# An attention and soft-MoE kernel: weight fetches behind the query stacks, and a new order of the first pair

## The chip, the cores and the metric

One core of one Trainium2 chip. The metric is the device time of one execution in microseconds (us). Engines: TensorE (PE, its weight loads PEld), VectorE (DVE), ScalarE (ACT), GpSimd (POOL) and SyncE (SP), which here only issues DMAs.

## The reference

Three layers follow each other, all in float32.

- Attention: q, k, v are 4 batches x 8 heads x 576 positions x 64. q and k are rotated (RoPE), then `softmax(q k^T / 8) v`.
- Soft MoE on the 2304 x 512 result x: `logits = x phi` (32 slots), softmax over the tokens for the dispatch and over the slots for the combine; 8 experts of 4 slots, each `relu(s w1) w2` with 512 x 1024 and 1024 x 512 weights.
- A feed-forward layer: `h = x w_in` (512 x 2048), `g = h tanh(softplus(h))`, `g w_out`.

## The kernel before, in words

The program is fully unrolled. It has an attention part (to about 325 us), a part for the experts (to about 370 us) and the feed-forward layer, whose second product fills the rest. The change touches the attention part alone.

**Pairs.** Attention runs over 16 pairs of heads (NP = 16), one after the other in a software pipeline. A pair has nine score tiles `S0` to `S8`: tile t of 128 queries of head h is number 2t + h, and S8 holds the last 64 positions of both heads. For each tile TensorE writes scores to PSUM (`S`, `scores` L375), VectorE takes the row maximum (`M`, `maxima` L383), ScalarE the exponential (`E`, `expo` L389), TensorE transposes it (`T`), ScalarE or VectorE copies it out (`t`), and TensorE multiplies by v (`A`, `B`). The pool `ps_s` (L79) has two score banks, so a score tile waits until the exponential of an earlier one has freed its bank. The pool `ps_m` (L80) has four banks for all else.

**High and low parts.** Scores are computed from two float32r parts of q and k, a high part (a rounded copy) and a low part (the rest), stacked on the 128 partitions. For pairs after the first, rotated q and k (GpSimd, `ropek`, `ropeq`) are transposed by TensorE (`Hk`, `Hq`, and `G` for the last 64 positions), ScalarE writes the high parts to the tile `parth` (`hka`, `hqa`, `ga`), VectorE the low parts to `partl` (`hkd`, `hqd`, `gd`), and DMAs from SBUF to SBUF carry them to their places in `qk_st` and `k2_st`: steps `dk` (eight DMAs) and `dq` (four), from `stack` L337. There is one buffer of `parth` and one of `partl`, so that `ga` (`rem_hi` L310), which is the first to write `parth` for the pair after, waits until all stacks that read it have landed.

**The first pair.** It has no stacks: the parts are written straight from PSUM (L718 to L773). `xk` holds both heads' transposed keys in one tile (heads on partitions 0 to 63 and 64 to 127) in one of the two score banks, `xq` the queries, `xr` the last 64 queries. `hi` (L728) is a ScalarE activation, `lo` (L731) a VectorE operation that needs the high part. Reads of one PSUM tile by two engines take turns in program order. `busy(n)` (L718) issues n filler matmuls.

**Order.** Each engine executes its instructions in the order in which the program issues them (class `InOrder`, L82). That order is written by hand: `PLAN` (L28) for each period, where `name@n` is the step for the pair n periods back, and `PLAN0` (L38) for the first pair. A step that issues to several engines takes its place in each of their queues. SyncE's queue carries nearly all DMAs: the stacks, the loads of q, k (`ld`) and v (`lv`), and, in most pairs, blocks of w_in and w_out that ScalarE, VectorE and GpSimd convert on the side (`ci` load, `Ca` ScalarE, `Cb` VectorE, `Cs` GpSimd, `co` store).

**The weight fetch.** Step `wf` (L820) is `fetch(ahead.pop(0), behind=True)`: one DMA of 1 MB of expert weights into a tile that nothing else uses by then, kept in its place in the order. It runs once a period for eight pairs, p = 2 to 9, as `wf@2`. In the old `PLAN` it stands between `hqa` and `Cb1`, so on SyncE's queue behind `dk` and in front of `dq`.

```python
             "wf": lambda p: fetch(ahead.pop(0), behind=True) if 2 <= p < 2 + NRA else None,
```

Of the kernel before, what the change touches and what calls it, by code (L numbers as in the profile page):

```python
# [27 lines left out]
PLAN = (  # L28
# [7 lines left out]


PLAN0 = (  # L38
    "E0 w3 Hk w3 ci1 S2 M2 S4 hka E2 M4 T0 S1 t0 E4 hkd M1 G S3 T2 ga E1 gd dk M3 S6 t2 E3 M6 T1 S5 E6 Hq t1 M5 "
    "T3 S7 hqa E5 hqd dq t3 M7 K0 S8 k0 E7 M8 A0 E8 ld:1 ropek:1 z0 A1 A2 ropeR:1 A3 A4 T4 ropeq:1 x0 t4 T5 "  # L40
    "ld:2 Y0 y0 t5"
).split()

# [5 lines left out]
def kernel(  # L49
# [14 lines left out]
    NB, H, S, D = q.shape  # L64
# [6 lines left out]
    SCALE = 1.0 / float(D) ** 0.5  # L71
# [282 lines left out]
    def s_mm(p, s, qc, h):  # L354
        st = qk_st[p % 2]
        for half in range(2):
            o = h * S + half * 288
            pe.matmul(s[:, half, 0:288], lhsT=st[:, qc:qc + 128], rhs=st[:, KC + o:KC + o + 288],
                      start=True, stop=False)
            pe.matmul(s[:, half, 0:288], lhsT=st[:, qc:qc + 128], rhs=k2_st[p % 2][:, o:o + 288],  # L360
                      start=False, stop=True)

    def s_mm2(p, s):
        st = qk_st[p % 2]
        for half in range(2):
            n = 0
            for o, qc in ((half * 288, QZ), (KB + half * 288, QBR)):
                for rhs in (st[:, KC + o:KC + o + 288], k2_st[p % 2][:, o:o + 288]):
                    pe.matmul(s[:, half, 0:288], lhsT=st[:, qc:qc + 128], rhs=rhs,
                              start=(n == 0), stop=(n == 3))  # L370
                    n += 1
# [3 lines left out]
    def scores(p, i):  # L375
        t, h = divmod(i, 2)
        s = sc[p, i] = ps_s.tile([128, 2, 512], F32, tag="s", name="s")
        if t < 4:
            s_mm(p, s, (QA, QB)[h] + t * 128, h)
        else:  # L380
            s_mm2(p, s)

    def maxima(p, i):  # L383
        if i == 0:
            stat[p] = [a4.tile([128, 10], F32, tag="nmax", name="nmax", bufs=2), zs[p % 2],
                       a4.tile([128, 10], F32, tag="rz", name="rz", bufs=2)]
        dve.tensor_reduce(out=stat[p][0][:, i:i + 1], in_=sc[p, i][:, :, 0:288], axis=AX.XY, op=ALU.max, negate=True)
# [322 lines left out]
    up, dn = slice(0, 64), slice(64, 128)  # L710
    xk = ps_s.tile([128, 2, 512], F32, tag="s", name="xk").rearrange("p a n -> p (a n)")
    xq = ps_m.tile([128, 512], F32, tag="m", name="xq")
    xr = ps_m.tile([128, R], F32, tag="m", name="xr")
# [4 lines left out]
    def busy(n):  # L718

        z = c_all[:, 0, 0:4].rearrange("p t s -> p (t s)")  # L720
        for _ in range(n):
            pe.matmul(none, lhsT=z, rhs=z, start=True, stop=True)
# [5 lines left out]
    def hi(out, ps, scale=1.0):  # L728
        act.activation(out=out, in_=ps, func=AF.Copy, scale=scale)

    def lo(out, ps, hi, scale=1.0):  # L731
        dve.scalar_tensor_tensor(out=out, in0=ps, scalar=scale, in1=hi.bitcast(F32), op0=ALU.mult, op1=ALU.subtract)
# [12 lines left out]
    ka, k2a = st[:, KC:KC + S], s2[:, 0:S]  # L745
    kb, k2b = st[:, KC + KB:KC + KW], s2[:, KB:KW]
    kf, k2f = st[:, KC + S:KC + KB], s2[:, S:KB]
    qa, qar, qb = st[:, QA:QA + 512], st[:, QAR:QA], st[:, QB:QB + S]
    hi(ka[up], xk[up, 0:S])
    hi(k2a[dn], xk[up, 0:S])  # L750
    hi(k2b[dn], xk[dn, 0:S])
    hi(kb[up], xk[dn, 0:S])
    hi(qa[up, 0:128], xq[up, 0:128], SCALE)
    hi(qa[up, 128:512], xq[up, 128:512], SCALE)
    lo(k2a[up], xk[up, 0:S], ka[up])
    lo(ka[dn], xk[up, 0:S], ka[up])
    lo(qa[dn, 0:128], xq[up, 0:128], qa[up, 0:128], SCALE)
    busy(9)
    scores(0, 0)
    lo(qa[dn, 128:512], xq[up, 128:512], qa[up, 128:512], SCALE)  # L760
    hi(qb[dn, 0:512], xq[dn, 0:512], SCALE)
    hi(k2f[dn], xk[dn, 512:S])
    hi(kf[up], xk[dn, 512:S])
    hi(qb[dn, 512:S], xr[dn])
    hi(qar[up], xr[up])
    maxima(0, 0)
    lo(kb[dn], xk[dn, 0:S], k2b[dn])
    lo(k2b[up], xk[dn, 0:S], k2b[dn])
    lo(kf[dn], xk[dn, 512:S], k2f[dn])
    lo(k2f[up], xk[dn, 512:S], k2f[dn])  # L770
    lo(qb[up, 512:S], xr[dn], qb[dn, 512:S])
    lo(qar[dn], xr[up], qar[up])
    lo(qb[up, 0:512], xq[dn, 0:512], qb[dn, 0:512], SCALE)  # L773
    for i in range(2):
        dma(out=phi_sb[64 * i:64 * i + 64, :, i], in_=phi.rearrange("(c h p) s -> h p c s", h=2, p=64)[i])
    load_v(1)
# [101 lines left out]
    begin = [((w + ":0").split(":")[0], int((w + ":0").split(":")[1])) for w in PLAN0]  # L878
    late_feed = [(n, 1) for n in ("G", "ga", "gd", "Hk")]
    steps["w3"] = lambda p: busy(3)  # L880
    for name, p in begin:
        steps[name](p)
    for period in range(1, NP + last):
        for name, n in plan:
            p = period - n
# [445 lines left out]
```

## Time and profile before

| | |
|---|---|
| median of 3 runs | 607.21 us (604.88 to 607.4) |
| the profiled execution's own time | 606.94 us |
| its span, first to last instruction | 604.8 us |
| TensorE busy | 584.4 us, 97% |
| VectorE, ScalarE, GpSimd busy | 383.9, 339.2, 218.2 us |
| bytes moved by DMA | 108.46 MB, 179 GB/s over the span |

Times in rows are microseconds from the span's start. A busy share is an average over stages; TensorE's matmuls are pipelined and drawn longer than the distance at which they follow each other. "idle before <- X" names what ended an engine's idle time, as inferred from semaphores; a DMA's time to landing counts from its issue.

### The profile page before, as it was taken

The numbers are of one execution on the slowest core, as the hardware profiler recorded it, in microseconds if no ns is written. First come the engines' busy times: TensorE is split into PE (matmuls) and PEld (weight loads), VectorE is DVE, ScalarE is ACT, GpSimd is POOL, SyncE is SP. The second block draws the span as 40 slices with busy tenths as digits, with TensorE's granted clock in tenths as the row PEclk, the third lists the DMA queues.
The fourth block names the chain that finished last, engine by engine and source line by source line (L and its number), as shares of the span: only waits on it lengthen the run. The fifth ranks groups of instructions, "written<-read, shape, count | busy, mean of one in ns | idle before, by whom it ended". The sixth has DMA issues, their size and how long they took to land.

```text
span 604.8 us, 11027 instructions
## 1 busy us (share of the span) xinstructions
PE 584.4 (97%) x3949; PEld 461.2 (76%) x3949; DVE 383.9 (63%) x813; ACT 339.2 (56%) x778; POOL 218.2 (36%) x267
## 2 busy tenths in 40 slices
PE   8899999999999999999998989999999999999996
PEld 7688887877878787787875435778788888888885
DVE  6688888977869786887654243887865333433332
ACT  4688887877879686886761023767662111222221
POOL 4967889578875877673000300000000000000000
PEclk9999999999999999999998999999999999999999
DMA  8598789989999889769759798424002000210004
GB/s 230 148 249 223 218 233 288 272 242 257 267 265 242 243 259 276 203 172 299 258 216 362 268 388 354 174 98 147 2 29 77 0 1 0 68 37 1 2 1 104
DMA packets 59398, 108.46 MB, mean 179 GB/s; under 512 B 13008, under 2 KB 25424, under 8 KB 58832
## 3 DMA queue, kind: packets, MB, share of 16 engines
q1 hardware_dynamic: 59072, 107.50, 60.3%
q8 instruction: 31, 0.51, 0.4%
q10 hardware_dynamic: 272, 0.26, 0.1%
q14 instruction: 23, 0.19, 0.1%
HBM read 70.25 MB, written 9.96 MB: 133 GB/s over the span
## 4 chain that ended last, share of the span: by engine, by line
PE 74%; DMA 5%; DVE 3%; ACT 1%; POOL 1%; issue 1%; SPq 0%; DVEq 0%; ACTq 0%
PE o_ps L1215 32%; PE s L90 9%; PE m_av L90 9%; PE t L90 6%; PE hp L1181 3%; DMA qk_st<-parth 3%; PE h_ps L1008 2%; PE so_ps L1077 2%; PE warm L583 2%; PE m_lg L90 1%; DMA qk_st<-partl 1%; PE m_x L90 1%; PE m_si L90 1%; DMA w<-in_q_dram 1%; PE m_q L90 1%; PE m_wp L1158 1%
## 5 line engine op out<-in xcount | busy, mean ns | idle before, releaser
L90 DVE TENSOR_REDUCE nmax<-s 128x1 f32<-128x576 f32 x144 | 106.8, 751 | 24.9 <-PE s L90 22.9
L90 ACT ACTIVATE P<-s,nmax 128x576 f32<-128x576 f32 x144 | 107.1, 745 | 18.1 <-DVE nmax L90 16.3
L1215 PE MATMUL o_ps<-wo_h,gh 128*128 128x512 f32 x288 | 113.0, 392 | 0.0
L1215 PE MATMUL o_ps<-wo_l,gh 128*128 128x512 f32 x288 | 113.0, 392 | 0.0
L90 PE MATMUL s<-qk_st 128*128 128x288 f32 x320 | 102.6, 337 | 5.7 <-ACT P L90 5.0
L1188 ACT ACTIVATE room<-hp 128x512 f32<-128x512 f32 x72 | 43.0, 599 | 106.6 <-PE hp L1181 102.0
L1215 PE MATMUL o_ps<-wo_h,gl 128*128 128x512 f32 x288 | 100.8, 391 | 0.9 <-DVE gl L1196 0.9
L90 PE MATMUL s<-k_st,qk_st 128*128 128x288 f32 x320 | 89.3, 295 | 0.0
L90 POOL TENSOR_TENSOR w<-w,cs 128x512 f32<-128x512 f32 (+2 forms) x75 | 87.6, 1187 | 4.4 <-DMA w<-in_k_dram 2.3
L90 PE MATMUL t<-cs,P 128*128 128x128 f32 x576 | 84.2, 273 | 0.4 <-ACT P L90 0.4
L90 PEld LDWEIGHTS s<-qk_st 128*128 128x128 f32 x320 | 60.3, 188 | 21.7 <-ACT P L90 9.5
L90 POOL TENSOR_TENSOR w<-w 128x256 f32<-128x256 f32 (+2 forms) x86 | 65.4, 781 | 18.5 <-ACT P L90 15.9
L1190 DVE CAST gh<-room 128x512 fp32r<-128x512 f32 x49 | 20.9, 427 | 79.4 <-ACT room L1188 79.3
L90 PEld LDWEIGHTS t<-cs,P 128*128 128x128 f32 x576 | 68.1, 142 | 1.5 <-ACT P L90 0.7
L90 ACT COPY PT<-t 128x512 f32<-128x512 f32 (+1 forms) x111 | 60.9, 557 | 12.9 <-PE t L90 12.1
L1215 PEld LDWEIGHTS o_ps<-wo_h,gl 128*128 128x128 f32 x288 | 54.0, 188 | 13.2 <-DVE gl L1196 1.7
L1215 PEld LDWEIGHTS o_ps<-wo_l,gh 128*128 128x128 f32 x288 | 54.4, 189 | 9.0 <-DVE wo_l L1068 0.2
L1215 PEld LDWEIGHTS o_ps<-wo_h,gh 128*128 128x128 f32 x288 | 54.1, 188 | 9.2
L90 PEld LDWEIGHTS s<-k_st,qk_st 128*128 128x128 f32 x320 | 60.6, 190 | 0.0
L1196 DVE TENSOR_TENSOR gl<-room,gh 128x512 fp32r<-128x512 f32 x72 | 49.6, 690 | 4.6
L90 PE MATMUL m_av<-PT,w 128*64 128x320 f32 (+1 forms) x384 | 52.0, 411 | 0.0
L90 POOL TENSOR_TENSOR c_all<-c_all,tmp 128x64 f32<-128x64 f32 (+1 forms) x44 | 21.6, 490 | 53.0 <-DVE tmp L90 51.2
(171 smaller groups left out, 843.4 us busy)
## 6 DMA issues: line engine op xcount, KB each, us to landing
w<-in_moe_w_dram SPq DMA_DIRECT2D x23, 1024.0 KB, 8.0
w<-in_moe_w_dram SPq DMA_DIRECT2D x36, 256.0 KB, 5.4
w<-in_moe_w_in_dram SPq DMA_DIRECT2D x16, 512.0 KB, 5.5
qk_st<-parth SPq DMA_DIRECT2D x45, 144.0 KB, 5.3
qk_st<-partl SPq DMA_DIRECT2D x45, 144.0 KB, 5.5
room<-in_moe_w_out_dram SPq DMA_DIRECT2D x12, 512.0 KB, 3.5
w<-in_q_dram SPq DMA_DIRECT2D x16, 256.0 KB, 3.8
w<-scr_in SPq DMA_DIRECT2D x4, 1024.0 KB, 6.4
```

The lines of the kernel that those rows point to most:

```text
L90: return lambda *a, **k: tc.keep_in_program_order(f(*a, **k))
L583: tc.keep_in_program_order(nc.tensor.matmul(ps, lhsT=ident, rhs=ident, start=True, stop=True))
L1008: tc.keep_in_program_order(nc.tensor.matmul(h_ps[32 * g:32 * g + 32, fh, :], lhsT=si_t[:, c, 32 * e:32 * e + 32], rhs=rows[g][:, cc * F1 + ...
L1077: tc.keep_in_program_order(nc.tensor.matmul(so_ps[32 * g:32 * g + 32, :], lhsT=h_t[eg][:, c, 32 * g:32 * g + 32], rhs=parts[2, e, hf][0][: ...
L1158: pin(nc.tensor.matmul(ps[32 * c:32 * c + 32, :], lhsT=s_t[:, c, :], rhs=wi[:, c, :], start=True, stop=True))
L1181: pin(nc.tensor.matmul(hp[:, x, :], lhsT=wst[:, f * 128:(f + 1) * 128], rhs=ct[:, i * 256:(i + 1) * 256], start=True, stop=True))
L1188: pin(nc.scalar.activation(out=gg, in_=hp, func=AF.Mish))
L1190: pin((nc.scalar.copy if 0 < u < NG * GR else nc.vector.tensor_copy)(gh, gg))
L1196: pin(nc.vector.tensor_tensor(out=gl, in0=gg, in1=gh.bitcast(F32), op=ALU.subtract))
L1215: pin(nc.tensor.matmul(ops[i, n], lhsT=g_[:, cols], rhs=w_[f], start=(j == 0 and (x, k) == (0, 0)), stop=(j == NG - 1 and all(y[0] != n fo ...
```

## The change

- In `PLAN`, `wf@2` moves from behind `hqa` to behind `dq`.
- In the first pair's code, head 0's low parts come directly after head 0's two high parts; head 1's high parts follow behind S0, and the filler matmuls in front of S0 go from nine to six.
- The rest of head 1's parts becomes six steps of `PLAN0`: `hx` and `hr` (high parts of the last keys and queries), `lk`, `lf`, `lr`, `lq` (low parts of keys, last keys, last queries, queries).
- `PLAN0` takes the score tiles in the order 0, 2, 4, 6, 1, 3, 5, 7, 8 where it had 0, 2, 4, 1, 3, 6, 5, 7, 8. The second `w3` (three filler matmuls) moves from in front of S2 to behind S4, `ci1` from in front of S2 to behind S6, and the other steps keep their places around the tiles they belong to.

```diff
@@ -28,7 +28,7 @@
 PLAN = (
     "S0 y0@1 Cs0@1 E8@1 ropek@-1 hka t5@1 M0 Z@2 ci0 T6@1 hkd S1 R@1 zz@2 K1@1 ropeR@-1 co0@1 dk "
     "M1 t6@1 E0 rA@1 rD@1 E1 X0@1 k1@1 w0@1 ca0@1 T7@1 S2 t7@1 Ca1@1 Hq Q@1 M2 S3 M3 qD@1 hqa "
-    "wf@2 Cb1@1 qA@1 B0@1 E2 B1@1 E3 B2@1 B3@1 B4@1 D@1 S4 z1@1 x1@1 hqd Ca0 Cs1@1 T3 M4 X1@1 dq "
+    "Cb1@1 qA@1 B0@1 E2 B1@1 E3 B2@1 B3@1 B4@1 D@1 S4 z1@1 x1@1 hqd Ca0 Cs1@1 T3 M4 X1@1 dq wf@2 "
     "t3 w1@1 T0 S5 dD@1 M5 Y1@1 t0 y1@1 Cb0 co1@1 dA@1 lv@1 ca1@1 T2 T1 E4 rb@1 rc@1 rd@1 t2 S6 K0 T4 M6 ci1 E5 "
     "lC@1 t1 La S7 Lb ra k0 G@-1 t4 E6 A0 la z0 A1 lb ropeq@-1 ro A2 M7 A3 lA A4 x0 ga@-1 lB "
     "S8 ld@-2 gd@-1 T5 E7 M8 Y0 Hk@-1 "
@@ -36,8 +36,8 @@
 
 
 PLAN0 = (
-    "E0 w3 Hk w3 ci1 S2 M2 S4 hka E2 M4 T0 S1 t0 E4 hkd M1 G S3 T2 ga E1 gd dk M3 S6 t2 E3 M6 T1 S5 E6 Hq t1 M5 "
-    "T3 S7 hqa E5 hqd dq t3 M7 K0 S8 k0 E7 M8 A0 E8 ld:1 ropek:1 z0 A1 A2 ropeR:1 A3 A4 T4 ropeq:1 x0 t4 T5 "
+    "hx E0 lk lf w3 Hk S2 hr M2 S4 E2 M4 lr w3 hka E4 lq S6 ci1 S1 T0 hkd M6 G t0 M1 S3 T2 ga E6 gd dk E1 M3 t2 S5 E3 T1 "
+    "Hq t1 M5 T3 S7 hqa E5 hqd dq t3 M7 K0 S8 k0 E7 M8 A0 E8 ld:1 ropek:1 z0 A1 A2 ropeR:1 A3 A4 T4 ropeq:1 x0 t4 T5 "
     "ld:2 Y0 y0 t5"
 ).split()
 
@@ -748,29 +748,38 @@
     qa, qar, qb = st[:, QA:QA + 512], st[:, QAR:QA], st[:, QB:QB + S]
     hi(ka[up], xk[up, 0:S])
     hi(k2a[dn], xk[up, 0:S])
+    lo(k2a[up], xk[up, 0:S], ka[up])
+    lo(ka[dn], xk[up, 0:S], ka[up])
+    hi(qa[up, 0:128], xq[up, 0:128], SCALE)
+    hi(qa[up, 128:512], xq[up, 128:512], SCALE)
+    lo(qa[dn, 0:128], xq[up, 0:128], qa[up, 0:128], SCALE)
+    busy(6)
+    scores(0, 0)
+    lo(qa[dn, 128:512], xq[up, 128:512], qa[up, 128:512], SCALE)
     hi(k2b[dn], xk[dn, 0:S])
     hi(kb[up], xk[dn, 0:S])
-    hi(qa[up, 0:128], xq[up, 0:128], SCALE)
-    hi(qa[up, 128:512], xq[up, 128:512], SCALE)
-    lo(k2a[up], xk[up, 0:S], ka[up])
-    lo(ka[dn], xk[up, 0:S], ka[up])
-    lo(qa[dn, 0:128], xq[up, 0:128], qa[up, 0:128], SCALE)
-    busy(9)
-    scores(0, 0)
-    lo(qa[dn, 128:512], xq[up, 128:512], qa[up, 128:512], SCALE)
     hi(qb[dn, 0:512], xq[dn, 0:512], SCALE)
-    hi(k2f[dn], xk[dn, 512:S])
-    hi(kf[up], xk[dn, 512:S])
-    hi(qb[dn, 512:S], xr[dn])
-    hi(qar[up], xr[up])
     maxima(0, 0)
-    lo(kb[dn], xk[dn, 0:S], k2b[dn])
-    lo(k2b[up], xk[dn, 0:S], k2b[dn])
-    lo(kf[dn], xk[dn, 512:S], k2f[dn])
-    lo(k2f[up], xk[dn, 512:S], k2f[dn])
-    lo(qb[up, 512:S], xr[dn], qb[dn, 512:S])
-    lo(qar[dn], xr[up], qar[up])
-    lo(qb[up, 0:512], xq[dn, 0:512], qb[dn, 0:512], SCALE)
+
+    def head_1(what):
+        if what == "hx":
+            hi(k2f[dn], xk[dn, 512:S])
+            hi(kf[up], xk[dn, 512:S])
+        elif what == "hr":
+            hi(qb[dn, 512:S], xr[dn])
+            hi(qar[up], xr[up])
+        elif what == "lk":
+            lo(kb[dn], xk[dn, 0:S], k2b[dn])
+            lo(k2b[up], xk[dn, 0:S], k2b[dn])
+        elif what == "lf":
+            lo(kf[dn], xk[dn, 512:S], k2f[dn])
+            lo(k2f[up], xk[dn, 512:S], k2f[dn])
+        elif what == "lr":
+            lo(qb[up, 512:S], xr[dn], qb[dn, 512:S])
+            lo(qar[dn], xr[up], qar[up])
+        else:
+            lo(qb[up, 0:512], xq[dn, 0:512], qb[dn, 0:512], SCALE)
+
     for i in range(2):
         dma(out=phi_sb[64 * i:64 * i + 64, :, i], in_=phi.rearrange("(c h p) s -> h p c s", h=2, p=64)[i])
     load_v(1)
@@ -878,6 +887,7 @@
     begin = [((w + ":0").split(":")[0], int((w + ":0").split(":")[1])) for w in PLAN0]
     late_feed = [(n, 1) for n in ("G", "ga", "gd", "Hk")]
     steps["w3"] = lambda p: busy(3)
+    steps |= {n: lambda p, n=n: head_1(n) for n in ("hx", "hr", "lk", "lf", "lr", "lq")}
     for name, p in begin:
         steps[name](p)
     for period in range(1, NP + last):
```

## Rows read from the trace of the kernel before

**Rows 1.** The page's chain by engine; windows table (busy us, clock, transfers, GB/s).
```profile
PE 74%; DMA 5%; DVE 3%; ACT 1%; POOL 1%; issue 1%; SPq 0%; DVEq 0%; ACTq 0%
...
130.00:155.00 25.00, 23.92 (x190) 19.17 (x187) 18.78 (x43) 19.78 (x48) 17.55 (x23) 1.00 0.98 248
```

**Rows 2.** Waits of ScalarE, 80 to 260 us (total, times, longest); its timeline.
```profile
ACT parth L90 <- DMA qk_st<-partl: 4.2, 2, 2.4
ACT parth L90 <- DMA qk_st<-parth: 3.2, 3, 1.5
...
143.00 0.37 ACT L90 CAST parth<-m_rem 128x256 fp32r<-128x256 f32 x1 [1.81 <-DMA qk_st<-partl]
```

**Rows 3.** Timeline of TensorE (start, us, ..., idle before and what ended it).
```profile
84.72 0.61 PE L90 MATMUL m_k<-cs,w 128*128 128x128 f32 x4
85.08 0.38 PE L90 MATMUL s<-qk_st 128*128 128x288 f32 x1
...
144.16 0.40 PE L90 MATMUL s<-qk_st 128*128 128x288 f32 x1 [0.92 <-ACT P L90]
...
145.56 0.40 PE L90 MATMUL s<-qk_st 128*128 128x288 f32 x1 [0.15 <-DMA w<-in_q_dram]
...
181.85 0.66 PE L90 MATMUL m_k<-cs,w 128*128 128x128 f32 x4 [0.58 <-ACT lt L90]
...
182.75 0.40 PE L90 MATMUL s<-qk_st 128*128 128x288 f32 x1 [0.24 <-ACT P L90]
...
240.90 0.40 PE L90 MATMUL s<-qk_st 128*128 128x288 f32 x1 [1.49 <-ACT P L90]
...
242.50 0.40 PE L90 MATMUL s<-qk_st 128*128 128x288 f32 x1 [0.36 <-ACT P L90]
```

**Rows 4.** Timeline of SyncE, DMA issues from 131.9 us on.
```profile
131.91 0.62 SPq L154 DMA_DIRECT2D w<-in_moe_w_dram  x1
132.63 0.84 SPq L90 DMA_DIRECT2D qk_st<-parth  x1
```

**Rows 5.** DMA issues: KB each, us to landing; issued at 134.16, at 76.50.
```profile
qk_st<-parth SPq DMA_DIRECT2D x1, 144.0 KB, 8.7
...
qk_st<-parth SPq DMA_DIRECT2D x1, 144.0 KB, 4.4
```

**Rows 6.** Conversion loads issued at 182.44 and 174.78 (us to landing); ScalarE's readers.
```profile
w<-in_moe_w_in_dram SPq DMA_DIRECT2D x1, 512.0 KB, 7.2
...
w<-in_moe_w_in_dram SPq DMA_DIRECT2D x1, 512.0 KB, 9.0
...
186.62 1.23 ACT L90 ACTIVATE w<-w 128x512 f32<-128x512 f32 x2
...
190.74 1.26 ACT L90 ACTIVATE w<-w 128x512 f32<-128x512 f32 x2
```

**Rows 7.** First pair, timelines: three rows of ScalarE, three of VectorE, two of TensorE.
```profile
10.16 0.65 ACT L90 ACTIVATE qk_st<-xk 64x576 fp32r<-64x576 f32 x1
...
18.14 0.74 ACT L90 ACTIVATE P<-s,nmax 128x576 f32<-128x576 f32 x1 [2.48 <-DVE nmax L90]
...
27.74 0.74 ACT L90 ACTIVATE P<-s,nmax 128x576 f32<-128x576 f32 x1 [0.73 <-DVE rz L90]
...
10.84 0.75 DVE L90 SCALAR_TENSOR_TENSOR k_st<-xk,qk_st 64x576 fp32r<-64x576 f32 x1 [1.01 <-ACT qk_st L90]
...
15.77 0.23 DVE L90 SCALAR_TENSOR_TENSOR qk_st<-xk,k_st 64x64 fp32r<-64x64 f32 x1
...
17.35 0.76 DVE L90 TENSOR_REDUCE nmax<-s 128x1 f32<-128x576 f32 x1
...
12.60 0.40 PE L90 MATMUL s<-qk_st 128*128 128x288 f32 x1
...
19.02 0.40 PE L90 MATMUL s<-qk_st 128*128 128x288 f32 x1 [1.49 <-ACT P L90]
```

**Rows 8.** Windows table, end of the attention part (TensorE first, then granted clock).
```profile
326.00:330.00 4.00, 4.00 (x24) 3.72 (x24) 1.30 (x5) 1.25 (x5) 0.00 (x0) 0.63 0.94 280
```

## The prediction

> **What bounds the kernel now.** I read first the chain that ended last: TensorE has 74% of it and transfers 5% [rows 1]. So TensorE is the bound, and the question is where it pauses. The windows table says the same of one stretch in the attention part: TensorE busy 23.92 of 25 us, the transfers busy 0.98 of the time at 248 GB/s [rows 1]. Third, the waits of ScalarE between 80 and 260 us: the copy into `parth` waited five times for stack transfers, 4.2 + 3.2 = 7.4 us [rows 2]. That copy is step `ga`: it writes the tile that the stack transfers of the pair before still read, so it must wait for the last of them. The timeline shows one: 1.81 us, ended by a landing at 143.0 [rows 2].
>
> Fourth, what this costs TensorE. Undisturbed, the four transposes of `m_k` are drawn 0.61 us long, but the next matmul starts 0.36 us after their start, so each pause is drawn 0.25 us too short [rows 3]. Three of the five waits show beside a pause: 0.92 + 0.15 at 144.16 and 145.56, 0.58 + 0.24 at 181.85 and 182.75, 1.49 + 0.36 at 240.90 and 242.50, together 3.74 us. With 6 x 0.25 = 1.5 that makes **5.2 us**. The two other waits cost next to nothing. The chain is ACT: `ga` waits, the exponential queued behind it (E7) is late, it still holds one of the two score banks, and the next pair's S0 cannot be written.
>
> Fifth, why the stack lands late. SyncE issues the 1 MB weight fetch at 131.91, then the four q stacks from 132.63 on [rows 4]. The one for head 1, issued at 134.16, landed 8.7 us later; its like at 76.50, in a pair without a fetch, took 4.4 us [rows 5]. So transfers issued behind the megabyte wait for it.
>
> **The change, part by part.**
>
> *The fetch behind `dq` (eight pairs).* Nothing is added; one DMA moves past four others on SyncE's queue. The q stacks then follow the k stacks directly. Landing after 4.4 instead of 8.7 us, the third would be there at about 138, some 3 us before `ga` wants it (143.00 - 1.81 = 141.19). All five waits go: **-5.2 us**. Bounds: nothing, if the stacks are as late for another reason, and -5.2, since no more TensorE time is shown to hang on it. I take the whole, because every wait shown ended on just these transfers.
>
> What is late next: four DMA slots are passed by the fetch, 4 x 0.65 us = 2.7 us of SyncE's issue time. Behind it now as before stand the conversion store, the v load, the next conversion load and the q/k loads of a later pair. The same bytes are ahead of all of them in either order, so they move only by what the DMA engines idle in those 2.7 us. Stores and v have most of a pair's time (about 19 us) to spare. The conversion loads have less: the block issued at 182.44 landed after 7.2 us, at 189.6, and ScalarE reads it at 190.74 (slack 1.1); the one issued at 174.78 landed after 9.0, at 183.8, and is read at 186.62 (slack 2.8) [rows 6]. When the pause at 181.85 goes, ScalarE comes some 1.3 us earlier and the first slack is used up. I charge **+0.7 us** for that and its like; bounds 0 (the engines never idle) and the slower rival below. No engine but ScalarE is queued behind such a wait; behind it stand copies and exponentials, that is, TensorE's next score bank.
>
> *The first pair's parts in turns.* Before, ScalarE reads the key bank `xk` four times, the last from 10.16 to 10.81, and only then does VectorE start its low part, at 10.84, after 1.01 us of idling [rows 7]. With head 0's two reads first, VectorE can start when its rotation ends: 10.84 - 1.01 = 9.83. Two low parts of 0.75 and the first query tile's (estimated at half of one, 0.37) end at 11.7: S0 0.9 us earlier than 12.60 [rows 7]. Three filler matmuls leave; they ran in that wait, and cost nothing.
>
> From 11.4 on ScalarE makes five high parts of head 1 (two of 0.65, three shorter, estimated at 0.9 together) ahead of E0: 13.6. VectorE does head 1's key parts (0.75 + 0.75 + 2 x 0.23, from 13.7 to 15.65) and then M2, which before stood behind the query parts too, until 17.35. From M2 to E2 it is 0.8 us, so E2 goes from 18.14 to about 16.4: 1.7 us gained [rows 7].
>
> *Head 0's four tiles ahead.* S6 takes E2's bank at 17.3, E4 runs at 17.65, and S1 waits for E4's bank until 18.5. The transposes T0 stand behind S1 on TensorE, so ScalarE, which has `t0` next in its order, idles from 18.4 to 19.8: 1.4 us lost. After that exponentials and tile copies alternate as before, with S3 held until E6 ends (21.4) and M5 behind the copy t1. Carried on in this way (an exponential 0.74 long, its bank free 0.88 after its start, 18.14 to 19.02; from a maximum to its exponential 0.8), E8 comes out at 28.1, against 27.74 in the trace [rows 7]. The same working, applied to the old order, gives 27.7. TensorE is dense from there on, so **+0.4 us**. Bounds: -1.7 (what E2 gained is kept) and +1.5 (the idle stretch is not made up by anything). I take the worked value, since it reproduces the old order.
>
> The bank turn is where a rule speaks against the change. The Trainium skill, "PSUM — Partial Sum Buffer", section "PSUM bank collisions raise a hardware error", says that two engines collide on one bank only within the same 32-partition quadrant. By it, VectorE's read of partitions 0 to 63 need not have waited for ScalarE's read of 64 to 127, and the new order would gain nothing at S0, about 603.7 in all. The row shows the wait all the same (the turn is the program's, by bank), so the sum goes by the row.
>
> **Sum.** The profiled execution took 606.94 us (span 604.8, 2.1 around it), 0.27 below the median of 607.21. 606.94 - 5.2 + 0.7 + 0.4 = **602.8**. About 0.5% (3 us) is what a measurement of this kernel can tell from no change: the limits are 604.2 and 610.2.
>
> **Rivals.**
>
> *The transfers themselves are the bound.* For it: the engines are busy 0.98 of the time at 248 GB/s, and the bytes stay the same. Then shorter pairs make the queue deeper, the k stacks ahead of the q stacks land later, and half of the 5.2 us returns at `ga` or at the loads: 606.94 - 2.6 + 0.4 = 604.7, no change. Against it: pairs without a fetch also show busy engines, and their stacks land in half the time.
>
> *Conversion loads hold ScalarE: slower.* Suppose that the loads behind the fetch are later by its whole length, 1.05 MB at 248 GB/s = 4.2 us. Eleven conversion loads fall in the fetch pairs. With slacks of 2.8 for ten and 1.1 for one, ScalarE waits 10 x 1.4 + 3.1 = 17.1 us; of the `ga` waits 5.2 of 7.4, or 0.7, reached TensorE, so 12.0. Time: 606.94 - 5.2 + 0.4 + 12.0 = 614.1. It decides from a delay of about 3.3 us on, where 0.7 x (11 d - 29.1) reaches the 4.8 gained. Against it: the loads already stand behind the fetch.
>
> *The clock falls in the first pair.* For it: after a sparse stretch at the end of attention the granted clock of 326 to 330 was 0.63, that is, partly the lower level of 1.2 GHz [rows 8]; the new order leaves TensorE sparse work from 12 to 21 us. By the row, 0.37 of 4 us is lost, 1.5 us: 604.3. Against it: in the old order TensorE idled 1.49 us before 19.02, and its first matmul after that took 0.40 us, as at 12.60 [rows 7]. The Trainium skill, "TensorE: Matmul & The Clock Gate", section "What's actually happening", has a gate that follows how busy the engine has been; by it removing filler matmuls is a risk, and the time would be that of this rival.
>
> **How the numbers follow.** Forecast 0.62 (its own range 601 to 604.2), transfers bound 0.23, clock 0.08, slower rival 0.07. The forecast lies under 604.2 but for a small part, which a small part of the clock's case balances: faster 0.62, no change 0.31, slower 0.07. The low end, 600.6, takes the prologue's lower bound (602.8 - 2.1). The high end, 606.4, takes in both unchanged cases with the prologue's upper bound (604.7 + 1.1, and some of the spread of the runs); left out are the slower rival and about a tenth at the edges.
>
> **What would show it.** Right: the fetch after the fourth q stack; q stacks landing in 4 to 6 us; no wait of `parth` on stack transfers between 80 and 260 us; S0 near 11.7, E2 near 16.4, E8 near 28.1. Wrong: pauses of TensorE at the pairs' ends that now end on other transfers; ScalarE's conversion steps waiting for their load; a clock under 1.00 before 25 us; E8 before 27.7, which would make the prologue a gain.

## The result, and the profile after

The changed kernel takes **599.79 us** in the median of four runs (599.69 to 599.93), the kernel before 606.96 beside it (four runs, 604.88 to 607.4): a ratio of 0.9889 [0.9866, 0.9912]. The forecast was 602.8 with a range of 600.6 to 606.4. The direction is right; the time lies 0.8 us below the range, so the prediction of the time is wrong. The profiled execution took 599.69 us (span 597.6), 7.25 less than the one before.

The changed kernel's page, the chain that ended last, by engine (to rows 1):

```profile
PE 80%; DVE 2%; ACT 1%; issue 0%; POOL 0%; DVEq 0%; ACTq 0%
```

Transfers had 5% of that chain [rows 1] and have none now. The waits of ScalarE between 80 and 260 us, changed kernel (to rows 2; total, times, longest), every row that names `parth` or a transfer:

```profile
ACT parth L90 <- PE m_q L90: 0.5, 2, 0.3
ACT w L90 <- DMA w<-in_moe_w_in_dram: 0.2, 1, 0.2
```

The 7.4 us for which the copy into `parth` waited on stack transfers [rows 2] are gone. What is left waits on TensorE, and the conversion loads, for which the prediction charged 0.7 us, hold ScalarE once for 0.2.

SyncE's timeline of the changed kernel, one pair with a fetch (to rows 4), and then its DMA issues of 95.2 to 96.4 and 96.5 to 96.6 (KB each, us to landing; to rows 5):

```profile
95.91 0.59 SPq L90 DMA_DIRECT2D qk_st<-partl  x1
96.54 0.59 SPq L154 DMA_DIRECT2D w<-in_moe_w_dram  x1
```

```profile
qk_st<-partl SPq DMA_DIRECT2D x2, 144.0 KB, 4.2
qk_st<-parth SPq DMA_DIRECT2D x1, 144.0 KB, 4.1
...
w<-in_moe_w_dram SPq DMA_DIRECT2D x1, 1024.0 KB, 6.6
```

The fetch is issued directly behind the last q stack. The stacks land after 4.1 to 4.2 us where the one behind the fetch took 8.7 [rows 5]. In the eight fetch pairs the last three q stacks take 2.8 to 4.4 us.

TensorE's timeline of the changed kernel at three ends of pairs, those of 144, 182 and 241 us before (to rows 3), and at a later one:

```profile
142.46 0.61 PE L90 MATMUL m_k<-cs,w 128*128 128x128 f32 x4
142.82 0.38 PE L90 MATMUL s<-qk_st 128*128 128x288 f32 x1
...
179.29 0.60 PE L90 MATMUL m_k<-cs,w 128*128 128x128 f32 x4
179.66 0.38 PE L90 MATMUL s<-qk_st 128*128 128x288 f32 x1
...
235.54 0.61 PE L90 MATMUL m_k<-cs,w 128*128 128x128 f32 x4
235.91 0.38 PE L90 MATMUL s<-qk_st 128*128 128x288 f32 x1
...
272.85 0.61 PE L90 MATMUL m_k<-cs,w 128*128 128x128 f32 x4
```

The score matmul follows its `m_k` group after 0.36 to 0.37 us at all three, the undisturbed distance. The same `m_k` group is a good mark of how far ahead one kernel is of the other, because the work between two marks is the same. Here are those behind the three pauses and the last one (TensorE's timelines, kernel before, then after):

```profile
162.25 0.61 PE L90 MATMUL m_k<-cs,w 128*128 128x128 f32 x4
...
200.88 0.61 PE L90 MATMUL m_k<-cs,w 128*128 128x128 f32 x4
...
260.07 0.61 PE L90 MATMUL m_k<-cs,w 128*128 128x128 f32 x4
...
278.57 0.61 PE L90 MATMUL m_k<-cs,w 128*128 128x128 f32 x4
```

```profile
160.44 0.61 PE L90 MATMUL m_k<-cs,w 128*128 128x128 f32 x4
...
197.77 0.61 PE L90 MATMUL m_k<-cs,w 128*128 128x128 f32 x4
...
254.37 0.61 PE L90 MATMUL m_k<-cs,w 128*128 128x128 f32 x4
```

After minus before, mark by mark: +0.43 behind the first pair, still +0.42 at 85.14 (against 84.72 [rows 3]), -0.17 at 142.46, -1.81 at 160.44, -2.56 at 179.29 (against 181.85 [rows 3]), -3.11 at 197.77, -3.27 at 235.54, -5.70 at 254.37, -5.72 at 272.85. So the fetch pairs gave 0.42 + 5.72 = **6.14 us**: 1.64 + 1.30 + 2.43 = 5.37 at the three pauses that the prediction had counted, and 0.77 elsewhere.

From there to the end of attention the gap grows once more, to -7.25, and then stays within 0.05. The reason is the granted clock. Windows table of the same work, before, then after (stretch; length; busy us of PE, PEld, DVE, ACT, POOL; granted clock; transfers; GB/s; to rows 8):

```profile
326.00:329.00 3.00, 3.00 (x15) 2.88 (x15) 1.30 (x5) 1.25 (x5) 0.00 (x0) 0.50 0.98 274
```

```profile
320.00:323.00 3.00, 3.00 (x27) 2.67 (x26) 1.34 (x6) 1.25 (x5) 0.00 (x0) 1.00 0.98 360
```

Before, TensorE was granted 0.50, its lower level of 1.2 GHz, from 325.6 to 329.0; after, the full 2.4 GHz. Timeline, the same 16 matmuls, before and after:

```profile
326.20 3.37 PE L583 MATMUL warm<-cs 128*128 128x128 f32 x16
```

```profile
320.26 2.05 PE L583 MATMUL warm<-cs 128*128 128x128 f32 x16
```

7.25 - 5.72 = **1.5 us** came from that, 1.32 of it in these 16 matmuls. The time adds up: 606.94 + 0.43 - 6.14 - 1.54 = 599.69.

The first pair of the changed kernel, three engines (to rows 7):

```profile
9.70 0.74 DVE L90 SCALAR_TENSOR_TENSOR k_st<-xk,qk_st 64x576 fp32r<-64x576 f32 x1
...
11.59 0.38 PE L90 MATMUL s<-qk_st 128*128 128x288 f32 x1
...
16.36 0.74 ACT L90 ACTIVATE P<-s,nmax 128x576 f32<-128x576 f32 x1 [1.54 <-DVE nmax L90]
...
19.78 0.59 ACT L90 COPY PT<-t 128x512 f32<-128x512 f32 x1 [1.37 <-PE t L90]
...
28.17 0.74 ACT L90 ACTIVATE P<-s,nmax 128x576 f32<-128x576 f32 x1 [0.79 <-DVE rz L90]
```

VectorE no longer waits for ScalarE's reads before its first low part; S0 is 1.0 earlier and E2 1.8 earlier than before, and E8 is 0.43 later: the gain is lost in the 1.37 us for which ScalarE idles at `t0`, and behind it.

### The profile page after: what moved, and what is told of

Read it like the earlier page. It is cut to its first block, busy times and chain, and to the rows that moved or that the text cites. A ratio compares the mean times of both kernels' runs of the same rounds, so it can differ in the third digit from the quotient of the medians.

```text
span 597.6 us, 11016 instructions
## 1 busy us (share of the span) xinstructions
PE 580.5 (97%) x3943; PEld 459.4 (77%) x3943; DVE 385.1 (64%) x813; ACT 339.5 (57%) x778; POOL 218.9 (37%) x267
## 4 chain that ended last, share of the span: by engine, by line
PE 80%; DVE 2%; ACT 1%; issue 0%; POOL 0%; DVEq 0%; ACTq 0%
PE o_ps L1225 32%; PE s L90 11%; PE m_av L90 10%; PE t L90 7%; PE hp L1191 3%; PE h_ps L1018 2%; PE so_ps L1087 2%; PE m_lg L90 2%; PE warm L583 1%; PE m_x L90 1%; PE m_si L90 1%; PE tk L90 1%; PE m_q L90 1%; PE m_wp L1168 1%; PE m_k L90 1%; PE m_w L1174 1%
```

## The experiments

All but the orders a and b and their versions with fillers keep the code of one of the two kernels with a small edit. Times are medians. "Before" is the old kernel on the same chip.

### The two halves apart

The old kernel with the fetch alone moved:

```diff
-    "wf@2 Cb1@1 qA@1 ... X1@1 dq "
+    "Cb1@1 qA@1 ... X1@1 dq wf@2 "
```

> The old kernel with the weight fetch moved behind the q stacks, nothing else. Theory (the copy into parth waits for stacks that stand behind the megabyte): all five waits of ScalarE on stack transfers go, TensorE gets 6.1 us back between 85 and 279 us, and the execution takes 606.9 - 6.1 = 600.8 us, or 599.3 if the clock also stays up at the end of the attention part. Rival (the transfers are the bound): half of it, about 603.9, with waits that now end on other transfers. Rival (the gain needs the new first pair): no change.

Measured: 600.09 us (four runs, 599.7 to 601.74) against 607.05, ratio 0.9882 [0.9813, 0.9951]. No wait of `parth` on a transfer is left. The whole gain of the change is here, and the marks of its trace show it: its `m_k` group starts at 85.57 against 84.72 before, and at 273.31 against 278.57, so the fetch pairs gave 0.85 + 5.26 = 6.11 us. The slowest of the four, 601.74, is the profiled one; its granted clock was 0.50 in two stretches, one in the old first pair and one at the end of attention (windows table; TensorE's timeline, the 16 matmuls of above):

```profile
20.20:23.20 3.00, 3.00 (x13) 2.97 (x14) 1.43 (x3) 1.82 (x5) 2.92 (x4) 0.50 0.52 112
320.60:323.60 3.00, 3.00 (x15) 2.88 (x15) 1.30 (x5) 1.25 (x5) 0.00 (x0) 0.50 1.04 378
```

```profile
320.78 3.53 PE L583 MATMUL warm<-cs 128*128 128x128 f32 x16
```

So with the fetch moved and nothing else, the fall at the end of attention was still there in this execution.

The changed kernel with the fetch put back in front of `dq`, so that only the first pair is new:

```diff
-    "Cb1@1 qA@1 ... X1@1 dq wf@2 "
+    "wf@2 Cb1@1 qA@1 ... X1@1 dq "
```

> The changed kernel with the weight fetch put back in front of the q stacks: only the first pair is new. Theory: the first pair ends 0.4 us later, the five waits are all there again, and the time is 606.9 + 0.4 = 607.3, that is, no change from before. Rival (the first pair brings part of the gain, through the clock or through what follows): 605.5 or less.

Measured: 608.48 (ten runs, 606.89 to 612.38) against 607.05, ratio 1.0037 [1.0003, 1.007]. So the first pair's new order alone gains nothing. The median is 1.4 us above the old kernel's; the first pair explains 0.43 of that by the marks above, and the rest was not taken apart. The waits are back (ScalarE's waits, 80 to 260 us; three more, which the view puts down to other DMAs, make 11.1 us where the old kernel had 7.4), and so is what they do to TensorE (its timeline):

```profile
ACT parth L90 <- DMA qk_st<-parth: 6.5, 3, 3.4
```

```profile
243.30 0.61 PE L90 MATMUL m_k<-cs,w 128*128 128x128 f32 x4
246.37 0.40 PE L90 MATMUL s<-qk_st 128*128 128x288 f32 x1 [2.47 <-ACT P L90]
```

The windows around this pause show its second price:

```profile
243.00:246.00 3.00, 0.91 (x9) 0.67 (x7) 0.00 (x0) 0.79 (x2) 2.92 (x3) 1.00 1.07 259
247.00:250.00 3.00, 3.00 (x14) 2.68 (x13) 2.79 (x6) 2.53 (x6) 2.84 (x5) 0.50 0.59 209
```

TensorE was busy 0.91 of 3 us, and directly behind that, with TensorE fully busy again, the clock was 0.50. So one late stack cost the pause (3.07 - 0.36 = 2.7 us) and then a stretch at 1.2 GHz.

### Which part of the first pair's change costs

The changed kernel with its parts in turns, but the score tiles in the old order 0, 2, 4, 1, 3, 6, 5, 7, 8:

```diff
-    "hx E0 lk lf w3 Hk S2 hr M2 S4 E2 M4 lr w3 hka E4 lq S6 ci1 S1 T0 hkd M6 G t0 M1 S3 T2 ga E6 gd dk E1 M3 t2 S5 E3 T1 "
-    "Hq t1 M5 T3 S7 hqa E5 hqd dq t3 M7 K0 S8 k0 E7 M8 A0 E8 ld:1 ropek:1 z0 A1 A2 ropeR:1 A3 A4 T4 ropeq:1 x0 t4 T5 "
+    "hx E0 lk lf w3 Hk w3 ci1 S2 hr M2 S4 lr lq hka E2 M4 T0 S1 t0 E4 hkd M1 G S3 T2 ga E1 gd dk M3 S6 t2 E3 M6 T1 S5 E6 Hq t1 M5 "
+    "T3 S7 hqa E5 hqd dq t3 M7 K0 S8 k0 E7 M8 A0 E8 ld:1 ropek:1 z0 A1 A2 ropeR:1 A3 A4 T4 ropeq:1 x0 t4 T5 "
```

> The changed kernel with the old order of the score tiles (0, 2, 4, 1, 3, 6, 5, 7, 8) and the parts still taken in turns. Theory (the turns gain, and the new tile order gives it back because T0 stands behind S1 on TensorE and ScalarE idles): the exponential E8 of the first pair starts at 26.6 instead of 28.2 us and the time is 599.8 - 1.5 = 298.3 + 300.0 = 598.3. Rival (the turns alone gain nothing): E8 at 27.7 or later, 599.4 or more.

Measured: 599.35 (598.54 to 600.27) against 607.05, ratio 0.9873 [0.9814, 0.9932]. Two runs at 598.5 and 598.6 had a mean clock of 0.998, two at 600.1 and 600.3 one of 0.995. Its E8 in the trace:

```profile
27.00 0.74 ACT L90 ACTIVATE P<-s,nmax 128x576 f32<-128x576 f32 x1 [0.74 <-DVE rz L90]
```

That is 0.74 earlier than before [rows 7] and 1.17 earlier than with four tiles of head 0 first. So at E8 taking the parts in turns gains 0.7 us, and the new tile order loses 1.2. I had expected E8 at 26.6 and 598.3 us (the sum of the expectation should read 599.8 - 1.5 = 598.3): E8 came 0.4 later, and only the two runs with the higher clock are near that time.

Two orders of my own were worked out with the durations of rows 7, for the same steps. Order a takes the score tiles 0, 2, 4, 6, 1, 3, 5, 8, 7, order b 0, 2, 4, 1, 6, 3, 5, 7, 8. Behind `E8` and `A0` both go on as the changed kernel does.

```diff
-    "hx E0 lk lf w3 Hk S2 hr M2 S4 E2 M4 lr w3 hka E4 lq S6 ci1 S1 T0 hkd M6 G t0 M1 S3 T2 ga E6 gd dk E1 M3 t2 S5 E3 T1 "
...
+    "hx lf lk E0 w3 Hk S2 M2 hr E2 S4 M4 w3 lq hka E4 G S6 ci1 T0 M6 S1 hkd ga S3 t0 gd dk T2 M1 M3 E6 lr E1 Hq S5 T1 "
+    "E3 M5 t2 t1 T3 hqa hqd dq E5 K0 t3 S8 S7 M7 E7 k0 M8 A0 E8 "
...
+    "hx E0 lk Hk w3 S2 lf hr M2 S4 w3 E2 lq M4 hka lr E4 T0 S1 G S6 ci1 M1 hkd M6 ga T2 S3 E1 t0 gd dk E6 M3 T1 S5 t1 "
+    "t2 Hq E3 M5 T3 K0 hqa S7 hqd dq M7 E5 t3 S8 k0 E7 M8 E8 A0 "
```

> The changed kernel with another order of the first pair: T0 ahead of S1, head 1's tiles between S6 and S5, and tile copies where ScalarE is free. Worked out with the same durations as in the prediction, the first product with v starts at 24.8 (27.2 in the changed kernel) and the stacks of the second pair have landed by 29.4 (31.8): 599.8 - 2.2 = 597.6. Rival (the second pair then waits for its stacks or rotations): within 0.5 us of the kernel with the old tile order, 599.0.

> The changed kernel with a third order of the first pair: S0, S2, S4, S1, S6, S3, S5, S7, S8 with T0 ahead of S1. Worked out as before: the first product with v at 24.9, E8 at 26.0, the stacks landed by 29.9: 599.8 - 2.1 = 597.7. Rival (the second pair waits for stacks or rotations): 599.0.

Measured: order a 599.17 (597.88 to 599.6), ratio 0.9858 [0.9802, 0.9913]; order b 598.18 (598.04 to 598.28), ratio 0.9845 [0.9791, 0.9899], both against 608.69. The first product with v, from which TensorE is dense, in order a and in order b (TensorE's timelines); after the change it starts at 27.20, before at 26.77, and the forecasts were 24.8 and 24.9:

```profile
24.78 1.95 PE L88 MATMUL m_av<-PT,v 128*64 128x256 f32 x16
```

```profile
25.41 1.95 PE L88 MATMUL m_av<-PT,v 128*64 128x256 f32 x16
```

Order a comes out as worked out, order b 0.5 later. Order a is the earlier one at that point and still the slower one at the end. The rival of the expectation, that the second pair waits, is not the reason: order a's 16 filler matmuls at the end of attention start at 318.17, where the changed kernel's start at 320.26, so 2.1 of the 2.4 us are still there. Order a's windows table says why:

```profile
318.20:321.20 3.00, 3.00 (x15) 3.00 (x15) 1.17 (x5) 1.24 (x5) 0.00 (x0) 0.50 1.02 369
```

Three of its four runs had a mean clock of 0.995; the one at 1.000 took 597.88.

### Is it the one buffer, or the transfers?

The old kernel with the fetch where it was, but with a second buffer for `parth` and `partl` up to the tenth pair (two weight tiles that are idle until then are lent to every other pair), so that `ga` need not wait for the stacks of the pair before:

```diff
+    lend = dict(zip("hl", (parts[key][0] for key in ahead[NRA - 2:NRA])))
...
-            part[x, p] = ae.tile([128, 2, 640], F32R, tag="part" + x, name="part" + x)
+            if p % 2 and p < 10:
+                part[x, p] = lend[x][:, 0:1280].bitcast(F32R).rearrange("p (a n) -> p a n", a=2)
+            else:
+                part[x, p] = ae.tile([128, 2, 640], F32R, tag="part" + x, name="part" + x)
```

> The old kernel, fetch in its old place, but the parts of the odd pairs up to 9 are written to two idle weight tiles instead of parth and partl, so that the copies of pairs 6, 8 and 10 (the waits at 103.5, 143.0 and 181.1 in the old profile) no longer write what the stacks in flight still read. Theory (the wait is for the buffer that the late stacks read): these three waits go though the stacks land as late as before; those at 200.2 and 239.8 stay; 0.6 + 1.6 + 1.3 = 3.5 us less, 603.4. Rival (TensorE's next score tiles wait for the stacks' data itself): the pauses at these places stay, within 0.5 us of before.

Measured: 607.91 (ten runs, 602.0 to 610.63) against 608.69, ratio 0.9976 [0.9933, 1.0019]: no gain that can be measured, where I had expected 603.4. (Three of the ten runs, 602.0 to 603.9, are faster than the fastest of the old kernel's 13 beside it, 604.53, so a gain in some executions is not excluded.) The lateness moved. ScalarE's and TensorE's timelines:

```profile
114.51 1.21 ACT L90 ACTIVATE w<-w 128x512 f32<-128x512 f32 x2 [2.10 <-DMA w<-in_moe_w_in_dram]
...
142.03 0.38 ACT L90 CAST parth<-m_rem 128x256 fp32r<-128x256 f32 x1
...
240.61 0.37 ACT L90 CAST parth<-m_rem 128x256 fp32r<-128x256 f32 x1 [3.73 <-DMA qk_st<-parth]
```

```profile
163.53 0.37 PE L90 MATMUL s<-qk_st 128*128 128x288 f32 x1 [1.36 <-DMA qk_st<-partl]
```

The copy at 142.03, which waited 1.81 us [rows 2], does not wait. But at 163.53 TensorE itself now waits for the stacked data, and ScalarE waits 2.10 us for a conversion load. The wait of 3.73 belongs to the pairs from the tenth on, which share one buffer again. So in this execution the buffer was only the first to notice that the transfers are late.

The changed kernel with the fetch between head 0's and head 1's q stacks asks how far behind is far enough (`wf@2` leaves `PLAN`, and the step `dq` issues the fetch in the same eight periods):

```diff
+                    if nm == "q" and h == 0 and 4 <= p < 4 + NRA:
+                        fetch(ahead.pop(0), behind=True)
```

> The changed kernel with the fetch between head 0's and head 1's q stacks, so that only the last two stacks of a pair stand behind the megabyte. Theory (the copy into parth waits for the last stack that reads it): the waits stay, TensorE loses about 4 to 6 us as in the old order, 604 to 606. Rival (only the data of the next pair's first score tile matters): head 0's stacks land in time, no pauses, 599.8.

Measured: 610.44 (ten runs, 607.47 to 611.55) against 608.84, ratio 1.0024 [0.9998, 1.005]. All of the gain is gone. DMA issues of 153.5 to 154.9 and of 155.5 to 156.9, on either side of the fetch of 154.95:

```profile
qk_st<-parth SPq DMA_DIRECT2D x1, 144.0 KB, 3.2
qk_st<-partl SPq DMA_DIRECT2D x1, 144.0 KB, 3.1
...
qk_st<-parth SPq DMA_DIRECT2D x1, 144.0 KB, 7.9
qk_st<-partl SPq DMA_DIRECT2D x1, 144.0 KB, 7.5
```

In one queue, within 3 us, equal transfers land after 3.1 to 3.2 us ahead of the fetch and after 7.5 to 7.9 behind it. The readers wait for the last of the four (ScalarE's waits, 80 to 260 us):

```profile
ACT parth L90 <- DMA qk_st<-parth: 7.9, 3, 4.0
```

I had expected 604 to 606: less is lost, I thought, since two of the four stacks are early. The last of them decides.

### Fillers against the fall at the end of attention

The old kernel with six filler matmuls in front of the last logits of attention:

```diff
+    warm(ps_m, "m", 6)
```

> The old kernel with six filler matmuls ahead of the transposes of the last batch's logits, in the sparse stretch before the clock fell. Theory (the 1.5 us that the changed kernel gained between 316 and 326 us are the clock, which fell to 1.2 GHz in the old kernel's profile and not in the changed one's): the clock stays up, sixteen filler matmuls behind it take 2.05 instead of 3.37 us, and the time is 605.4. Rival (the fillers cost their own time, and the clock falls as before): 607 to 608.

Measured: 606.78 (ten runs, 604.47 to 610.55), ratio 1.001 [0.9976, 1.0043]. As a time this decides nothing. In the trace the 16 matmuls that took 3.37 us took 2.05, but the clock had fallen elsewhere, at 125.5, behind a pause of 2.5 us (windows table):

```profile
125.60:128.60 3.00, 3.00 (x16) 1.06 (x20) 2.47 (x5) 1.32 (x3) 2.92 (x3) 0.50 0.94 264
326.00:329.00 3.00, 3.00 (x27) 2.68 (x27) 1.67 (x6) 0.57 (x1) 0.00 (x0) 1.00 1.02 378
```

The fillers were then added to order b and to order a, whose pairs have no pauses.

> The kernel before this one (third order of the first pair) with six filler matmuls ahead of the last batch's logits. Theory (what spread is left in kernels without the waits is the clock, which falls in some executions in the sparse stretch at the end of the attention part and costs 1.5 us): all runs within 0.5 us of each other, at the lower end of the runs without the fillers, 597.7. Rival (the spread comes from elsewhere): some runs 1.5 us above the others as in the kernel with the old tile order.

> The kernel of the second order of the first pair (T0 ahead of S1, head 1's tiles between S6 and S5) with six filler matmuls ahead of the last batch's logits. Without them three of its four runs took 599.0 to 599.6 us and one 597.9, and its profile shows the clock at 1.2 GHz from 318.0 to 321.4. Theory (the clock at the end of the attention part is the whole spread): all runs at 597.9 within 0.3 us, no fall there. Rival (the fillers do not hold the clock, or the spread comes from elsewhere): runs at 599.0 or more remain.

Measured: order b 598.23 (598.08 to 598.32), ratio 0.9846 [0.9791, 0.99]. It had no fall without them either, so this run says only that they cost nothing. Order a: **597.75** (597.45 to 598.09), ratio 0.9838 [0.9807, 0.9869] against 608.84; its four mean clocks were 0.999 or 1.000 where three of order a's four were 0.995. The stretch that ran at 0.50 without them:

```profile
317.00:320.00 3.00, 3.00 (x27) 2.68 (x27) 1.57 (x6) 0.66 (x2) 0.00 (x0) 1.00 1.01 382
```

This version is the best of the study: 11.1 us below the old kernel beside it, where the change itself was 7.2 below (2.0 us between their medians, from two series). It has the fetch behind `dq`, the parts in turns, order a, and six fillers.

## Why the prediction was wrong, point by point

**What bounds the kernel: right.** The late stacks held `ga`, and through the exponential and its score bank TensorE: -5.2 was forecast for three pauses, and they gave 5.37. With the fetch alone moved the waits and the pauses go, with it put back they return, and with it two transfers earlier they return too.

**The step that failed: the sum 606.94 - 5.2 + 0.7 + 0.4, with -5.2 as a bound "since no more TensorE time is shown to hang on it".** Two things were missing in it. "The two other waits cost next to nothing" was one: the marks give 0.77 us in the fetch pairs outside the three pauses, and 5.37 for the three themselves. The larger one is the clock, which had no term in the sum. I had read the low clock at the end of attention [rows 8] and used it only as a price for the first pair; in the sum of the old time it was left in, as if it stayed. In the profiled execution of after it is not there, 1.54 us. That is not shown to be the change's doing: the same move alone still has the fall in its profile (320.60 to 323.60 above), and so has order a (318.20 to 321.20). With the fall the profiled execution would have taken 599.69 + 1.54 = 601.2 us, inside the range. So what failed is that the sum took over one execution's clock, with neither a term nor a bound for a fall that comes in some executions and not in others.

Pauses of the kind that the move removes can bring such falls too: one stands behind the pause at 243.30 above, and one each behind pauses of 2.5 and 3.4 us in two other profiles (fillers in the old kernel, behind 122.50; fetch between the heads, behind 241.97). The pauses at 144, 182 and 241 of the kernel before had none behind them (clock 1.00 from 95 to 250 in the windows table below), so no share of the 7.25 us comes from there.

**"+0.7 for conversion loads": did not occur.** The only wait on them is 0.2 us, and TensorE shows no pause there. The load whose slack was 1.1 us did not come later but earlier: issued at 180.66 in the changed kernel, it landed after 4.2 us where it had taken 7.2 [rows 6], and ScalarE reads it at 187.63, 2.8 us after the landing (DMA issue; ScalarE's timeline).

```profile
w<-in_moe_w_in_dram SPq DMA_DIRECT2D x1, 512.0 KB, 4.2
```

```profile
187.63 1.26 ACT L90 ACTIVATE w<-w 128x512 f32<-128x512 f32 x2
```

The error is the sum: 1.54 (clock) + 0.7 (loads) + 0.77 (outside the three pauses) + 0.17 (5.37 against 5.2) - 0.03 (first pair) is 3.15, and 602.84 - 599.69 is 3.15. Two small sums of the prediction are off by 0.1 (4 x 0.65 is 2.6, and 602.8 - 2.1 is 600.7); nothing hangs on them.

**The first pair: right.** S0 at 11.59 for a forecast of 11.7, E2 at 16.36 for 16.4, `t0` at 19.78 for 19.8, E8 at 28.17 for 28.1; +0.43 us for +0.4. ScalarE idles at `t0` for 1.37 us as forecast. The old tile order with the new turns takes the +0.43 apart: -0.74 for the turns, +1.17 for the tile order.

**The rivals.** *Transfers are the bound*: wrong for this place. Over the fetch pairs the transfers were about as busy as before and the gain came all the same; it was the order in the queue that counted, not the amount. Windows tables, before and after (columns as above; the transfers' share is 0.94, then 0.93):

```profile
95.00:250.00 155.00, 150.65 (x1203) 122.15 (x1202) 121.57 (x274) 120.47 (x299) 117.56 (x138) 1.00 0.94 259
```

```profile
95.00:245.00 150.00, 149.44 (x1213) 122.81 (x1213) 123.99 (x276) 121.66 (x301) 118.25 (x138) 1.00 0.93 268
```

*The clock falls in the first pair*: not in the changed kernel's profile. It can happen, but in either order: the clock fell there in the profiles of both halves apart, one of which has the old first pair. *Conversion loads hold ScalarE*: no. *The bank rule*: VectorE began at 9.70 instead of 10.84 once it had its turn first, so the wait was the program's, as the row said.

Of the Trainium skill's "TensorE: Matmul & The Clock Gate", section "What's actually happening", the traces agree that the clock follows how busy TensorE has been: 0.50 directly behind 0.91 busy us of 3. They do not say when it falls: the same sparse stretch at the end of attention had a fall in some profiles and none in others. The Trainium skill, "DMA: Bandwidth & Descriptors", section "Queues, rings and completion order", states that each DMA engine consumes the descriptors of a ring in order. The traces agree, as far as landings tell: 7.5 to 7.9 us behind the fetch, 3.1 to 3.2 ahead of it.

## What to carry to other kernels

In one DMA queue, put the transfers that the next step waits for ahead of the bulk ones that have time; with two of a set of four left behind nothing was gained here, and a second buffer moved the wait to the next reader. Price a long pause of TensorE (here those of 2.5 to 3.4 us) with the stretch at half clock that can follow it (a fall cost 1.5 us where it was measured, at the end of attention), and look in the windows table for such stretches in the old kernel before you take its time as the base of a sum: one that comes only in some executions belongs in the bounds. Where an order is written by hand, work it out with the trace's own durations: that gave the changed first pair to 0.1 us and the later orders to 0.5 or better, and it found orders that start TensorE's dense work 1.8 to 2.4 us earlier.

## What was not expected

With the fetch in its old place the time varies more from one execution to the next. In one series 18 runs of the old kernel took 602.68 to 610.84 us; after the change four runs lie within 0.24. The other versions with the fetch behind `dq` spread over 0.2 to 2.1 us (four runs each), those with it ahead of q stacks over 4.1 to 8.6 (ten runs each). The old kernel's time goes with its mean granted clock (from the results of that series):

```
mean clock          runs   us, lowest to highest   mean us
0.997 and above     7      602.68 to 607.05        605.1
0.994 to 0.995      4      604.25 to 608.28        606.3
0.993 and below     7      607.40 to 610.84        608.9
```

The mean clock of the first group is 0.998, of the last 0.991; 0.007 of 605 us is 4 us, about the 3.8 between the groups. None of these runs has a profile, so this is read from the means alone: it fits that the old kernel's executions differ mostly in how often the clock falls (some 1.5 us each time), and it does not show it. In the profiles shown here the clock falls behind pauses or sparse stretches of TensorE. Why a transfer behind the fetch is late by more in one execution than in another stays open, and so does why the four runs of the changed kernel, as far as their mean clocks of 0.998 to 1.000 tell, never fell at the end of attention while others with the same steps there did.
